# The order of all five instruction lists made anew in a chunk-selecting attention and ELU layer kernel

## The chip, the cores and the metric

The kernel runs on one core of one Trainium2 chip. The metric is the device time of one execution in microseconds, taken as the median of several runs. The engines of the core are called by short names: PE (TensorE, matmuls and transposes), ACT (ScalarE), DVE (VectorE), POOL (GpSimd) and SP (SyncE, which here only issues transfers). ACT and POOL issue transfers too, and such an issue is an instruction in the engine's own stream. Each engine works through its instructions in the order in which they stand and waits where an instruction needs what another engine or a transfer has not yet done.

## The reference

The first half is attention for 4 batches of 8 heads with 768 positions and 64 dimensions, in which each query attends to the six best of its allowed chunks of 32 keys:

```
k_min, k_max = min and max of each chunk of 32 keys
ub = sum(max(q * k_min, q * k_max), over the head's dimensions)
ub = where(chunk is not in the query's future, ub, -1e9)
top = the 6 chunks with the greatest ub
scores = where(key in a top chunk and not in the future, q @ k.T / 8, -1e9)
attn = softmax(scores);  x = attn @ v
```

The second half is a layer on the 3072 tokens with 512 features: `h = x @ w_in` (2048 wide), `g = where(h > 0, h, exp(min(h, 0)) - 1)`, and the result is `g @ w_out`, 3072 x 512 in float32.

## The kernel before, in words

Two heads make a pair; there are 16 pairs, four to a batch, and two pairs make a quad for the selection. Queries go in halves of 384. For a pair, k and q are brought into a layout with the head's 64 dimensions on the partitions, twice 64 for the two heads. DVE reduces each chunk of keys to its minimum and maximum; PE makes the bound `ub` from them (line 782); DVE finds the sixth greatest of each query (line 810) and marks the chunks below it (line 814), transposes the marks, and POOL puts them as extra rows below q (line 832). The extra rows of k hold an expanded identity times -40000, `econ` (line 531), copied there by DVE (line 542), so that one matmul (line 874) gives scores with the unwanted chunks pushed far down. ACT takes the exponential (line 901), PE multiplies with v (line 933), DVE divides by the sum (lines 946 and 949), PE transposes (line 982) and ACT copies the result into the tile xT (line 985). The second half takes xT: an up-projection in 16 pieces of 128 features (line 1011), the nonlinearity on ACT and DVE (lines 1020 to 1054), a down-projection (line 1070), a copy (line 1079) and a store (line 1084).

The first batch is prepared differently, to start early. `first_prep` loads k and q of a pair and half of the queries in plain rows (`load`, line 674) and v (line 679); PE transposes them, six instructions for a tile (`turn`, line 696), and ACT copies the transposed tiles out of PSUM (line 706 for k, 728 and 732 for q), while DVE reduces k from PSUM (line 715). Loads of k go through the queue of SP. The four loads of q for the first half of the queries are issued by ACT, all others of this batch by SP:

```
early = u - SPLIT[0] < EARLY[hf]
fetch(1, 256, 768, (pl + 0.1) - 300.0 * early, load(i0 + 1, qr, nc.scalar if early else nc.sync), [(sg, i0 + 1)],
      eng="ACT" if early else "SP")
```

The order of the work is written out by hand. The program first lists 1720 operations with what they read, write, allocate and free (`plan.add`), each with a number in the order of listing. The table `QUEUE` holds, for each of the five engines, these numbers in the order in which the engine is to do them. `Plan.order` walks through the five lists with assumed durations, latencies and transfer rates, and gives one common order and the buffer that each allocation takes; in that order the program is emitted (line 1115 and after), and semaphores are set between the engines from the tiles that they touch. The transfers of the SP and ACT queues share eight semaphores, used in turn in the order in which the built program has the transfers; a transfer whose semaphore is still in use by the transfer eight places earlier waits until that one has landed. The order of the built program follows the emission within each engine, while how ACT's and SP's transfers are put among each other also depends on what the building library takes the instructions of the two engines to last.

PSUM is shared out in banks: four banks are taken in turn by the transposed tiles, the up-projections, the outputs of attention and the down-projections (class `ps`, with counts for each kind), and two pairs of banks by the scores (class `S2`).

Of the kernel before, what the change touches and what calls it, by code (L numbers as in the profile page):

```python
# [73 lines left out]
    ],  # L74
    "POOL": [
# [10 lines left out]
    ],  # L86
    "ACT": [
# [19 lines left out]
    ],  # L107
# [7 lines left out]
    ],  # L115
# [1037 lines left out]
```

## Time and profile before

| what | before |
|---|---|
| median of 3 runs | 268.43 us (268.42 to 268.64) |
| span of the profiled execution | 266.7 us |
| PE busy | 256.0 us, 96% of the span |
| DVE busy | 211.6 us, 79% |
| ACT busy | 195.8 us, 73% |
| POOL busy | 118.0 us, 44% |
| moved by transfers | 32.15 MB, mean 121 GB/s |

A row of a stretch gives, for each engine, the time in which at least one of its instructions ran and their number. A row of the timeline gives start, duration, engine, line, operation, the tiles written and read, their shape, how many instructions are merged in it, and in brackets how long the engine had been idle and what ended that. "SPq" and "ACTq" are transfers issued by these engines. The matmuls overlap in PE, so the duration of one is longer than the distance to the next. The profiled execution's span is 1.7 us under the median of the runs.

### The profile page before, as it was taken

Reading aid. Unit: us, or ns where it says so; the run is one execution under the profiler, and the core shown is the slowest. Engines: PE = TensorE matmul, PEld = TensorE weight load, DVE = VectorE, ACT = ScalarE, POOL = GpSimd, SP = SyncE. Lnnn points to the kernel's source line nnn. Section 1 sums busy time; section 2 is a strip of 40 time slices with the busy share of each in tenths; the row PEclk is TensorE's granted clock in tenths of the full one; section 3 lists DMA queues with packets and bytes.
Section 4 is the critical chain, followed back from the end, with each engine's and each line's share of the span. In section 5 each row is a group of like instructions: output and inputs, shape, how many; then the busy total and the mean of one; then the engine's idle time right before and its main releaser. Section 6 shows DMA issues by size and latency. Waiting matters only on the chain.

```text
span 266.7 us, 6618 instructions
## 1 busy us (share of the span) xinstructions
PE 256.0 (96%) x2393; PEld 159.4 (60%) x2420; DVE 211.6 (79%) x544; ACT 195.8 (73%) x363; POOL 118.0 (44%) x208
## 2 busy tenths in 40 slices
PE   4999999999999999999999999999999999999994
PEld 3887766755565556655565555655666555565543
DVE  4897999999999999899997858986779676227640
ACT  4899899955987789997899549787988842433421
POOL 2588774163896898952934157524250000000000
PEclk9999999999999999999999999999999999999999
DMA  6999999999998999999403561040102300210123
GB/s 206 272 238 155 205 194 202 196 147 177 198 153 134 163 204 159 152 167 186 106 7 77 175 172 18 15 125 15 58 11 59 116 2 0 79 42 0 39 81 118
DMA packets 121264, 32.15 MB, mean 121 GB/s; under 512 B 108304, under 2 KB 118288, under 8 KB 121232
## 3 DMA queue, kind: packets, MB, share of 16 engines
q1 hardware_dynamic: 115920, 26.75, 51.3%
q0 software_dynamic: 4224, 4.19, 10.0%
q10 hardware_dynamic: 1088, 0.79, 0.9%
q8 instruction: 19, 0.31, 0.5%
q14 instruction: 13, 0.11, 0.2%
HBM read 28.44 MB, written 7.47 MB: 135 GB/s over the span
## 4 chain that ended last, share of the span: by engine, by line
PE 83%; DVE 5%; ACT 5%; DMA 4%; issue 2%; SPq 0%; DVEq 0%; ACTq 0%
PE psH L1011 20%; PE psM L1070 20%; PE psS L874 11%; PE psS L1011 8%; PE psMT L1070 8%; PE psO L933 7%; PE psS L782 3%; DMA f<-in_v_dram 3%; PE psH L696 2%; PE psMT L696 2%; ACT pt L901 2%; DMA gT<-in_k_dram 1%; ACT lhs L706 1%; PE psT L982 1%; DVE thr L810 1%
## 5 line engine op out<-in xcount | busy, mean ns | idle before, releaser
L901 ACT ACTIVATE pt<-psS 128x768 bf16<-128x768 f32 (+1 forms) x120 | 89.1, 778 | 11.9 <-PE psS L874 7.3
L1011 PE MATMUL psH<-xT,w_in_sb 128*128 128x384 bf16 x384 | 75.0, 326 | 0.3
L1070 PE MATMUL psM<-w_out_sb,gT 128*128 128x512 bf16 x264 | 67.9, 379 | 1.3
L1011 PEld LDWEIGHTS <-w_in_sb 128*128 128x128 bf16 x512 | 47.6, 97 | 34.4 <-issue 1.4
L1070 PEld LDWEIGHTS <-gT 128*128 128x128 bf16 x400 | 37.8, 98 | 34.4 <-DVE gT L1054 0.5
L1020 ACT ACTIVATE f<-psH 128x384 f32<-128x384 f32 x96 | 47.8, 509 | 12.5 <-PE psH L1011 10.1
L920 POOL TENSOR_SCALAR_AFFINE_SELECT pt<-pt 128x512 bf16<-128x512 bf16 (+1 forms) x48 | 24.8, 529 | 69.0 <-ACT pt L901 61.9
L874 PE MATMUL psS<-rhs,lhs 88*128 88x384 bf16 (+4 forms) x304 | 54.2, 283 | 0.8 <-ACT pt L901 0.6
L874 PEld LDWEIGHTS <-lhs 88*128 88x128 bf16 x304 | 27.9, 97 | 15.4 <-ACT pt L901 1.9
L1049 DVE SCALAR_TENSOR_TENSOR t<-f,psH 128x384 bf16<-128x384 f32 x56 | 30.5, 546 | 6.3 <-ACT f L1020 5.8
L748 POOL CAST rhs<-f 64x768 bf16<-64x768 f32 (+1 forms) x40 | 27.9, 702 | 14.1 <-DVE f L633 6.6
L933 PEld LDWEIGHTS <-pt 128*128 128x128 bf16 x672 | 27.5, 98 | 7.5 <-issue 0.9
L1054 DVE SCALAR_TENSOR_TENSOR gT<-psH,t 128x384 bf16<-128x384 f32 x56 | 30.6, 551 | 1.2
L933 PE MATMUL psO<-vext,pt 128*128 128x65 bf16 x672 | 29.6, 194 | 0.2 <-DVE gT L1054 0.2
L748 POOL CAST lhs<-f 64x768 bf16<-64x768 f32 x24 | 19.7, 822 | 18.6 <-PE psS L874 12.3
L832 POOL COPY rhs<-selt 24x576 bf16<-24x576 bf16 (+2 forms) x40 | 22.7, 567 | 8.6 <-DVE selt L821 5.8
L1020 ACT ACTIVATE f<-psS 128x768 f32<-128x768 f32 x16 | 13.0, 811 | 18.0 <-PE psS L1011 17.9
L1028 DVE SCALAR_TENSOR_TENSOR gT<-f,psH 128x384 bf16<-128x384 f32 x40 | 21.4, 542 | 5.3 <-ACT psH L1025 5.3
L1011 PE MATMUL psS<-xT,w_in_sb 128*128 128x384 bf16 x128 | 22.6, 326 | 0.0
L1070 PE MATMUL psMT<-w_out_sb,gT 128*128 128x512 bf16 (+1 forms) x109 | 22.1, 348 | 0.2
L1025 ACT ACTIVATE psH<-psH 128x384 f32<-128x384 f32 x40 | 20.7, 520 | 0.0
L949 DVE TENSOR_TENSOR on<-psO,rc 128x384 bf16<-128x384 f32 x32 | 17.6, 554 | 0.8
(56 smaller groups left out, 270.9 us busy)
## 6 DMA issues: line engine op xcount, KB each, us to landing
out_dram<-osb SPq DMA_DIRECT2D x23, 256.0 KB, 2.5
f<-in_k_dram SPq DMA_DIRECT2D x48, 96.0 KB, 3.9
f<-in_q_dram SPq DMA_DIRECT2D x48, 96.0 KB, 3.8
f<-in_v_dram SPq DMA_DIRECT2D x24, 192.0 KB, 4.0
w_in_sb<-in_moe_w_in_dram POOLq DMA_DIRECT2D x4, 512.0 KB, 7.9
w_out_sb<-in_moe_w_out_dram POOLq DMA_DIRECT2D x4, 512.0 KB, 8.4
gT<-in_k_dram SPq DMA_DIRECT2D x8, 192.0 KB, 4.4
gT<-in_v_dram SPq DMA_DIRECT2D x12, 128.0 KB, 3.9
```

Of the source, the lines that this page charges most:

```text
L748: nc.gpsimd.tensor_copy(out=o, in_=i)
L832: eng.tensor_copy(out=dst.rearrange("c h (i two x) -> c h i two x", two=2, x=32)[:, :, :, odd, :], in_=tiles[st][r0:r0 + NCH, c0:c0 + n].r ...
L874: nc.tensor.matmul(p_s[:, hd, pc:pc + w], lhsT=tiles[pt_["kb"]][0:64 + NCH, hd, 128 * kb:128 * kb + 128], rhs=tiles[pt_["qb"]][0:64 + NCH, ...
L901: lambda bs=bs, pt=pt, wtot=wtot, lo=lo, at=at: nc.scalar.activation(out=tiles[pt][:, :, lo:lo + wtot], in_=tiles[bs[0]][:, :, at:at + wto ...
L920: nc.gpsimd.affine_select(out=a, in_=a, compare_op=AOT.is_ge, fill=0.0, base=0, pattern=pat, channel_multiplier=-1)
L933: nc.tensor.matmul(po[:, hd, qi, :], lhsT=tiles[pt][:, hd, off:off + 128], rhs=tiles[pt_["vx"]][:, 6 * hd + kb, :], start=(kb == 0), stop= ...
L1011: nc.tensor.matmul(o, lhsT=w_in_sb[:, kk, f0:f0 + 128], rhs=rhs, start=(kk == 0), stop=(kk == NKK - 1))
L1020: lambda e=e, view=view: nc.scalar.activation(out=halves(e)[:, 0:step], in_=view(), func=AF.Exp),
L1028: lambda e=e, view=view, fc=fc, gt=gt: nc.vector.scalar_tensor_tensor(out=tiles[gt][:, fc:fc + step, :], in0=halves(e)[:, 0:step], scalar= ...
L1049: lambda e=e, t=t, view=view: nc.vector.scalar_tensor_tensor(out=tiles[t][:, 0:step], in0=halves(e)[:, 0:step], scalar=1.0, in1=view(), op ...
L1054: lambda t=t, view=view, fc=fc, gt=gt: nc.vector.scalar_tensor_tensor(out=tiles[gt][:, fc:fc + step, :], in0=view(), scalar=0.0, in1=tiles ...
L1070: nc.tensor.matmul(pm, lhsT=tiles[gt][:, fc, 128 * tt:128 * tt + 128], rhs=w_out_sb[:, fc, x0:x1], start=(fc == 0), stop=(fc == NFC - 1))
```

## The change: five new lists

All five lists of `QUEUE` are replaced. Each holds the same numbers as before, so every engine does the same operations, with the same shapes, on the same classes of buffers; the assumed lengths in `Plan` stay as they are. Of the 366 entries of ACT 339 stand elsewhere, of 562 of PE 528, of 382 of DVE 353, of 196 of POOL 180 and of 101 of SP 92; on average an entry moves by 4 (SP) to 9 (PE) places, at most by 55. The heads and tails of the lists show the kind of the moves:

```diff
     "ACT": [
-        15, 33, 49, 67, 2, 20, 21, 36, 37, 26, 27, 42, 43, 54, 55, 60, 61, 176, 70, 71, 177, 76, 77, 170, 171,
+        2, 33, 15, 49, 67, 20, 21, 36, 37, 42, 43, 70, 71, 26, 54, 27, 55, 60, 107, 108, 61, 76, 186, 187,
...
     "SP": [
-        13, 31, 163, 47, 65, 165, 17, 215, 181, 51, 217, 183, 197, 199, 201, 167, 517, 519, 534, 536, 551, 565,
+        13, 31, 163, 65, 47, 181, 183, 17, 165, 199, 215, 197, 51, 217, 519, 534, 167, 536, 517, 201, 551,
...
-        1341, 1704, 1697, 1711, 1718,
+        1270, 1658, 1644, 1263, 1355, 1697, 1711, 1704, 1718,
...
     "PE": [
-        19, 35, 25, 41, 53, 59, 175, 69, 81, 75, 169, 90, 185, 219, 191, 122, 203, 209, 106, 93, 131, 225, 147,
+        19, 35, 41, 69, 25, 53, 59, 106, 185, 75, 81, 90, 191, 169, 175, 122, 219, 147, 203, 131, 209, 225,
...
     "DVE": [
-        0, 6, 11, 9, 12, 8, 10, 22, 23, 38, 7, 39, 24, 40, 56, 57, 82, 72, 83, 73, 84, 172, 85, 58, 74, 188,
+        0, 8, 9, 11, 6, 12, 22, 10, 23, 24, 38, 39, 7, 40, 72, 73, 56, 57, 82, 83, 74, 84, 58, 188, 85, 189,
...
     "POOL": [
-        1, 5, 4, 3, 28, 29, 44, 45, 46, 62, 30, 63, 179, 78, 80, 79, 87, 64, 178, 86, 89, 195, 129, 194, 128,
+        1, 3, 5, 44, 45, 4, 28, 29, 30, 62, 46, 78, 79, 63, 195, 87, 64, 89, 194, 179, 178, 86, 88, 127,
```

In the ACT list 15, 33, 49 and 67 are the four loads of q, of pairs 0 to 3; 2 is econ; 20 and 21 copy the transposed k of pair 0, 36 and 37 that of pair 1. In the PE list 19 and 35 transpose k of pairs 0 and 1, 25 and 41 q of pairs 0 and 1, 53 and 69 k of pairs 2 and 3. In the SP list 13, 31, 47 and 65 load k of pairs 0 to 3, 17 is the first load of v, which has three parts, and the numbers from 163 to 217 are loads for the second half of the queries.

In the built program the first transfers stand as follows, with the semaphore that each waits for (the numbers in brackets are those of the lists; a value of 16 is one transfer landed, 32 two):

```
before                                   after
ACT q  (15)      no wait                 SP 13, 31, 163, 65, 47, 181, 183, and the
SP  k  (13)      no wait                    first part of 17: no wait (semaphores 0 to 7)
ACT q  (33)      no wait                 SP 17, parts 2 and 3    wait 0 >= 16, 1 >= 16
SP  k  (31)      no wait                 SP 165, 199             wait 2 >= 16, 3 >= 16
ACT q  (49)      no wait                 SP 215, 197             wait 4 >= 16, 5 >= 16
SP  k  (163)     no wait                 SP 51, part 1           wait 6 >= 16
ACT q  (67)      no wait                 ACT q (33)              wait 7 >= 16
SP  k  (47)      no wait                 SP 51, part 2           wait 0 >= 32
SP  k  (65)      wait 0 >= 16            ACT q (15)              wait 1 >= 32
SP  q  (165)     wait 1 >= 16            SP 51, part 3           wait 2 >= 32
SP  v  (17, 1)   wait 2 >= 16            ACT q (49)              wait 3 >= 32
...                                      ACT q (67)              wait 4 >= 32
```

On ACT itself the table load and econ stand first after the change, then the four loads of q, then the copies; before, the four loads stand first.

163 rows, old and new, of the table QUEUE are left out of this document.

## The prediction

> **What bounds the kernel now.** I read the page first, then the stretches by window, then the first microseconds as a timeline, engine by engine.
>
> ```profile
> span 266.7 us, 6618 instructions
> PE 256.0 (96%) x2393; PEld 159.4 (60%) x2420; DVE 211.6 (79%) x544; ACT 195.8 (73%) x363; POOL 118.0 (44%) x208
> PE 83%; DVE 5%; ACT 5%; DMA 4%; issue 2%; SPq 0%; DVEq 0%; ACTq 0%
> ```
>
> The profiled execution spans 266.7 us; the median of the three runs is 268.43 us, 1.7 us more, which lies around the span. I forecast a change of the span and add it to 268.43. TensorE (PE) is busy for 96% and makes 83% of the chain that ended last. What is left to win or lose is where PE is not the one that sets the pace. The stretches show where that is (columns: busy time of PE, PEld, DVE, ACT, POOL, then clock, DMA share and GB/s):
>
> ```profile
> 5.52:10.00 4.48, 4.46 (x26) 3.97 (x25) 4.45 (x14) 3.37 (x8) 1.25 (x3) 1.00 1.08 289
> 10.00:20.00 10.00, 9.54 (x150) 8.37 (x149) 8.44 (x38) 9.71 (x25) 7.73 (x18) 1.00 0.99 244
> 20.00:30.00 10.00, 9.25 (x180) 7.39 (x180) 8.27 (x45) 9.28 (x22) 8.93 (x18) 1.00 1.30 172
> 30.00:40.00 10.00, 9.79 (x100) 6.48 (x97) 9.52 (x18) 9.89 (x20) 7.05 (x13) 1.00 1.34 198
> 40.00:50.00 10.00, 9.95 (x93) 6.59 (x93) 9.47 (x20) 9.24 (x19) 4.15 (x6) 1.00 1.36 204
> 60.00:110.00 50.00, 49.39 (x462) 29.41 (x467) 49.44 (x129) 41.96 (x79) 38.68 (x60) 1.00 1.01 166
> 110.00:263.00 153.00, 152.01 (x1251) 89.53 (x1266) 111.09 (x251) 103.01 (x183) 44.05 (x73) 1.00 0.31 75
> 5.52:32.13 26.61, 25.34 (x377) 21.23 (x376) 23.25 (x99) 24.38 (x57) 19.73 (x39) 1.00 1.14 221
> ```
>
> Up to about 50 us ScalarE (ACT) is as full as PE: 9.71, 9.28, 9.89 and 9.24 us of each ten. From 60 to 110 us VectorE (DVE) is full, 49.44 of 50. After 110 us only PE is. So ACT is the engine that may not start late: what it loses at the start it can make up only from its own idle time. Between 5.52 us, its first copy of a transposed tile, and 32.13 us, the end of the copies that the first up-projection needs, that idle time is 26.61 - 24.38 = 2.23 us, of which 4.48 - 3.37 = 1.11 us lie before 10 us.
>
> The start itself, on ACT, then the load queue of SyncE (SPq), then PE:
>
> ```profile
> 0.80 2.06 ACTq L674 DMA_DIRECT2D gT<-in_q_dram  x4
> 2.90 1.28 ACT L531 ACT_TABLE_LOAD   x1 [2.90 <-issue]
> 4.20 0.84 ACT L531 ACTIVATE econ<-ident_f 32x768 bf16<-32x768 f32 x1
> 5.52 0.98 ACT L706 ACTIVATE lhs<-psH 64x384 bf16<-64x384 f32 x2 [0.48 <-PE psH L696]
> 30.66 1.47 ACT L985 ACTIVATE xT<-psT 128x384 bf16<-128x384 bf16 x3
> 31.44 1.71 PE L1011 MATMUL psH<-xT,w_in_sb 128*128 128x384 bf16 x8
> ```
>
> ```profile
> 4.29 0.37 SPq L674 DMA_DIRECT2D gT<-in_k_dram  x1
> 4.70 0.47 SPq L674 DMA_DIRECT2D gT<-in_q_dram  x1
> 5.42 0.37 SPq L679 DMA_DIRECT2D gT<-in_v_dram  x1
> 7.99 0.37 SPq L679 DMA_DIRECT2D gT<-in_v_dram  x1
> SPq L679 <- DMA gT<-in_q_dram: 1.9, 2, 1.6
> SPq L674 <- DMA gT<-in_q_dram: 1.5, 1, 1.5
> ```
>
> ```profile
> 3.96 2.79 PE L696 MATMUL psH<-ident_f,gT 128*128 128x128 f32 x12 [3.96 <-DMA gT<-in_k_dram]
> 9.13 0.85 PE L696 MATMUL psH<-ident_f,gT 128*128 128x128 f32 x6
> ```
>
> Two things are to be seen. ACT triggers four loads of q before anything else, free of any wait, and is done with that at 2.86 us. And no more than eight loads of the two queues are in flight: SP's load at 4.29 us is the ninth, and SP's rows of waits say that loads stood until an earlier load (of q) had landed, up to 1.6 us each. That is the built program's bookkeeping: eight semaphores used in turn, so that a load waits until the load eight places earlier has landed.
>
> **The change part by part.** Operations, shapes and tiles stay the same, so no duration is added or removed; only positions move. Four edits matter.
>
> *ACT's first five operations.* Before, the four q loads stand ahead of the expansion of the identity (econ, line 531); after, they stand behind it. In the built program that does more than the list says. While ACT loads its table (1.28 us) and makes econ (0.84 us), all eight semaphores go to SP's loads, and the four q loads become numbers 16, 18, 20 and 21 of the turn. The first waits for SP's 8th load, the second for its 10th, the third for its 12th, the fourth for its 13th. They are instructions of ACT, so every copy that ACT must make stands behind the fourth. When has SP's 13th load landed?
>
> ```profile
> gT<-in_k_dram SPq DMA_DIRECT2D x7, 192.0 KB, 4.0
> gT<-in_v_dram SPq DMA_DIRECT2D x4, 128.0 KB, 4.5
> DMA packets 4175, 2.34 MB, mean 234 GB/s; under 512 B 1601, under 2 KB 4175, under 8 KB 4175
> GB/s 0 0 0 0 0 0 0 58 49 240 221 320 369 363 375 363 372 301 255 273 280 301 286 258 249 320 363 366 363 363 356 351 318 306 269 224 203 206 236 170
> L674 ACTq DMA_DIRECT2D gT<-in_q_dram x4: 488/492/506, 0.8 to 2.4; - x4
> 10.00:11.00 1.00, 1.00 (x11) 1.00 (x10) 0.45 (x3) 0.97 (x2) 0.76 (x2) 1.00 1.01 273
> ```
>
> SP's first 13 loads are ten of 192 KB and three of 128 KB, together 2304 KB or 2.36 MB. In the trace of before the first 10 us moved 2.34 MB (the rows are for that stretch, in slices of 0.25 us), so the bytes alone take until 10.1 us. From the last byte to the end of the wait I take 0.8 us as an estimate: the slices sum to 0.4 MB, two loads, by 3.5 us, and the first waiting load went at 4.29 us. ACT's first two q loads are in flight by then and share the DMA engines; they are 0.39 MB, at 273 GB/s nothing to 1.4 us. The fourth trigger therefore goes between 10.9 and 12.3 us; I take the middle, 11.6. It takes 0.49 us itself, so ACT's first copy starts at 12.1 us instead of 5.52: 6.6 us later, with bounds 5.9 and 7.3.
>
> What hides it? Not another engine: the 61 ACT operations up to the last xT copy ahead of the first up-projection (line 1011, 31.44 us before) are the same set in both lists, so that row is due after the same ACT work. Of ACT's 2.23 us of idle time I let the early 1.11 us be made up (the transposes it waited for then will long be done) and keep the later 1.12 us, which came from waits for scores and selection that shift along. The delay at the first up-projection is 6.6 - 1.1 = 5.5 us.
>
> *PE's order behind that.* PE's third operation is now the transpose of the q tile that ACT's first held load brings, so PE stands from about 6.6 us (two groups of six transposes of k from 3.96 us, 2.79 us long) until that load lands, triggered near 7.8 us by the same byte count (SP's first eight loads, 1.5 MB, are reached at 7.0 us in the slices, and 0.8 us on top) and, at the 4 us from issue to landing of the rows above, landed near 12 us. From the fifth transpose on it needs PSUM banks that ACT's copies and DVE's reductions free, so ACT stays the later one; this costs nothing beyond the 5.5 us. Six transposes took 1.4 us in the first row of PE and 0.85 us at 9.13 us: the array may be slow again behind the gap, 0.55 us for each of the next two groups. They lie ahead of ACT's release, so I count 0, and 1.1 us for the upper end. [...]
>
> *DVE and POOL.* Econ is ready sooner (about 3 us instead of 5.04), so DVE's five copies of it, 2.77 us, run earlier:
>
> ```profile
> 5.07 2.77 DVE L542 COPY lhs<-econ 32x768 bf16<-32x768 bf16 x10 [2.71 <-ACT econ L531]
> 7.84 0.56 DVE L715 TENSOR_REDUCE km<-psH 128x12 f32<-128x384 f32 x1
> ```
>
> That saves nothing by itself, since the next operation, the reduction at 7.84 us, waits for ACT's second copy: 12.1 + 0.98 = 13.1 us, 5.3 us later than before. This is about the shift that PE sees, so DVE does not add to it. POOL (44% busy) waits for the same copies; 0, bounded by its idle time.
>
> *The rest of the five lists.* Most entries move by some five to nine places. After the first up-projection PE is idle for 0.21 + 0.05 us in the windows from 30 to 50, 0.61 us from 60 to 110 and 0.99 us from 110 to 263: 1.9 us is the most that a better order, or a delay taken up by waits that vanish, can give back; nothing is the least. I take 1.0. A loss here is possible where DVE is full (60 to 110 us), if its list asks for more before the same matmuls; I put 0 to 1.0 us, about the idle time seen there, and take 0. In the tail one store stands behind another that is ready later; the last matmuls, copies and the last store keep their order, so 0, up to 0.3 us.
>
> The sum: 6.6 - 1.1 - 1.0 = 4.5 us, 268.43 + 4.5 = 272.9 us.
>
> **The rivals.** *ACT is released early (the other side).* If the held loads cost ACT less than 2.2 us, that is if its first copy starts before about 7.7 us, its idle time takes it all, and the new order can win PE's idle time of 10 to 50 us, 0.46 + 0.75 + 0.21 + 0.05 = 1.5 us, and a little later: 266.9 us. For it speaks that q and k compete for the same engines and the sum of bytes is unchanged. Against it: 2.36 MB by 7.2 us would need 328 GB/s from the first instruction, and the trace has 234. [...] Chance 0.07.
>
> *The delay passes through whole.* ACT's waits all return at their old length and DVE, 5.3 us late, and the slow transposes add up to 1.1 us, with no gain later: 6.6 + 0 to 1.1, so 275.0 to 276.1 us. For it: up to 50 us both engines are over 90% full. Against it: 1.11 us of the idle time was waiting for the slow first transposes. Chance 0.2.
>
> *Most of it is taken up.* All of ACT's 2.23 us and PE's 1.9 us come back: 6.6 - 2.2 - 1.9 = 2.5 us, 270.9 us; with the early bound of the release 270.2. For it: the new lists could have been made with less waiting elsewhere. Against it: some of PE's idle is single gaps of 0.2 to 0.3 us that no order avoids. Chance 0.15.
>
> **How the numbers follow.** The forecast has 0.58 and its own range is 271.2 to 274.6 (release 10.9 to 12.3 us, idle made up between 1.1 and 3.0). The predicted time is 272.9 us. The range takes in the rivals on the slow side down to the early bound and up to the whole delay: 270.0 to 276.2. Outside stand the early release (0.07) and some 0.1 of worse cases. What a measurement of this kernel can tell from no change is about 0.2%, 0.54 us. Faster by more: 0.06; within: 0.03; slower: 0.91.
>
> **What would show it.** Right: the four q triggers on ACT come after econ and stretch to about 11 or 12 us, each behind a landing; ACT's first copy (line 706 moved by five) starts near 12 us; PE has a gap between about 6.6 and 12 us; the first up-projection starts near 37 us; behind 60 us PE is as full as before and the end comes about 4.5 us later. Wrong: the triggers go before 7 us, or the first up-projection starts near 37 us and the end is within 1 us of before, which would mean that PE's later time holds far more slack than its idle time shows; or losses of several us in the middle, which would mean that the order itself, not the start, decides.

## The result, and the profile after

| what | before | after |
|---|---|---|
| median | 268.43 us | 275.13 us (274.13 to 276.66, 4 runs) |
| profiled execution, its span | 268.4 us, 266.7 us | 274.13 us, 272.4 us |
| first up-projection starts | 31.44 us | 38.43 us |

The changed kernel is slower: the ratio of the times is 1.0248, with a 95% interval of 1.0207 to 1.0289. I had forecast 272.9 us in a range of 270.0 to 276.2; the sign and the range held, the value was 2.2 us too low. Two things make up most of that: the start lost 1.5 us more than I had summed, and the profiled execution, 274.13 us, lies 1.0 us under the median of the four. Where single executions of a kernel ran at a lower granted clock and some per cent longer than its others, the ratios below leave them out.

The page of the changed kernel has the same picture as before, with PE's share of the span down from 96% to 94% at the same busy time (255.5 us against 256.0):

```profile
span 272.4 us, 6614 instructions
PE 255.5 (94%) x2397; PEld 159.2 (58%) x2420; DVE 209.7 (77%) x544; ACT 194.4 (71%) x363; POOL 116.3 (43%) x208
```

So PE does no more work in all and stands longer. Where it stands is seen in the timeline of the start (start, duration, engine, line, operation, tiles, in brackets the idle time before and what ended it; all lines are five higher than before):

```profile
2.10 0.84 ACT L536 ACTIVATE econ<-ident_f 32x768 bf16<-32x768 f32 x1
3.60 2.79 PE L701 MATMUL psH<-ident_f,gT 128*128 128x128 f32 x12 [3.60 <-DMA gT<-in_k_dram]
...
8.43 3.39 ACTq L679 DMA_DIRECT2D gT<-in_q_dram  x4
11.86 1.99 ACT L711 ACTIVATE lhs<-psH 64x384 bf16<-64x384 f32 x4 [8.92 <-DMA gT<-in_k_dram]
12.94 0.56 DVE L720 TENSOR_REDUCE km<-psH 128x12 f32<-128x384 f32 x1 [6.76 <-issue]
13.27 1.54 PE L701 MATMUL psMT<-ident_f,gT 128*128 128x128 f32 x6 [6.88 <-DMA gT<-in_q_dram]
14.61 1.49 PE L701 MATMUL psH<-ident_f,gT 128*128 128x128 f32 x6
14.85 0.49 ACT L733 ACTIVATE f<-psMT 128x384 f32<-128x384 f32 x1 [1.00 <-PE psMT L701]
15.88 0.88 PE L701 MATMUL psMT<-ident_f,gT 128*128 128x128 f32 x6
16.13 0.98 ACT L711 ACTIVATE lhs<-psH 64x384 bf16<-64x384 f32 x2 [0.57 <-PE psH L701]
...
38.43 2.11 PE L1016 MATMUL psH<-xT,w_in_sb 128*128 128x384 bf16 x12
```

The view of waits for the first 40 us (engine, tile and line, waited for what: us in total, times, longest) gives two of these gaps their names:

```profile
ACT lhs L711 <- DMA gT<-in_k_dram: 8.9, 1, 8.9
PE psMT L701 <- DMA gT<-in_q_dram: 6.9, 1, 6.9
```

ACT makes econ and is done at 2.94 us. Its next instruction is the first trigger of a q load, which starts at 8.43 us; the four are through at 11.82 us, and only then come the copies of the transposed tiles, which had been waiting in PSUM since about 6.4 us. PE and DVE wait for the held load and the held copies. Behind the gap ACT waits twice more, 1.00 and 0.57 us, now for PE: the first two groups of six transposes there take 1.54 and 1.49 us.

Stretches of both kernels (length, then busy time and number of instructions of PE, PEld, DVE, ACT and POOL, then clock, DMA share, GB/s), of the changed kernel first: from ACT's first copy to its last xT copy, the middle, and from the first up-projection to the end. The last row is the kernel before from its first up-projection to the end.

```profile
11.86:38.54 26.68, 24.16 (x373) 20.40 (x374) 21.98 (x93) 24.24 (x57) 17.21 (x41) 1.00 1.18 180
60.00:110.00 50.00, 49.58 (x467) 29.48 (x471) 48.62 (x124) 39.75 (x72) 34.80 (x56) 1.00 0.99 153
38.43:272.00 233.57, 228.70 (x2018) 136.71 (x2038) 184.35 (x438) 168.18 (x306) 97.57 (x157) 1.00 0.57 105
```

```profile
31.44:266.70 235.26, 229.78 (x2016) 137.06 (x2040) 187.28 (x439) 169.84 (x307) 96.88 (x154) 1.00 0.57 108
```

The whole difference of the two spans can be laid out from these rows. ACT's first copy comes 11.86 - 5.52 = 6.34 us later. From there to the end of the last xT copy ACT takes 26.68 us, where it had taken 26.61 (the stretch from 5.52 to 32.13): 0.07 us more, with 57 instructions in both. The first up-projection starts 0.11 us ahead of that end, where it had started 0.69 us ahead: 0.58 us more. Then the rest takes 272.4 - 38.43 = 233.97 us instead of 235.26: 1.29 us less. The sum is 6.34 + 0.07 + 0.58 - 1.29 = 5.70 us, the difference of the two spans.

### The profile page after: what moved, and what is told of

The parts are those of the page before. It is cut to its first block, busy times and chain, and to the rows that moved or that the text cites. A ratio compares the mean times of both kernels' runs of the same rounds, so it can differ in the third digit from the quotient of the medians.

```text
span 272.4 us, 6614 instructions
## 1 busy us (share of the span) xinstructions
PE 255.5 (94%) x2397; PEld 159.2 (58%) x2420; DVE 209.7 (77%) x544; ACT 194.4 (71%) x363; POOL 116.3 (43%) x208
## 3 DMA queue, kind: packets, MB, share of 16 engines
HBM read 28.44 MB, written 7.47 MB: 132 GB/s over the span
## 4 chain that ended last, share of the span: by engine, by line
PE 88%; DMA 4%; ACT 3%; SPq 1%; DVE 1%; issue 1%; ACTq 0%; DVEq 0%
PE psH L1016 23%; PE psM L1075 22%; PE psS L879 13%; PE psO L938 7%; PE psMT L1075 6%; PE psS L1016 6%; PE psS L787 4%; PE psMT L701 2%; DMA gT<-in_q_dram 2%; PE psH L701 2%; ACT pt L906 2%; DMA gT<-in_v_dram 1%; PE psT L987 1%; SPq L679 1%; DMA out_dram<-osb 1%
## 5 line engine op out<-in xcount | busy, mean ns | idle before, releaser
L906 ACT ACTIVATE pt<-psS 128x768 bf16<-128x768 f32 (+1 forms) x120 | 89.8, 778 | 11.5 <-PE psS L879 10.5
L1075 PE MATMUL psM<-w_out_sb,gT 128*128 128x512 bf16 x267 | 69.7, 379 | 1.2 <-issue 0.2
L1025 ACT ACTIVATE f<-psH 128x384 f32<-128x384 f32 x96 | 46.7, 505 | 13.3 <-PE psH L1016 11.6
L879 PE MATMUL psS<-rhs,lhs 88*128 88x384 bf16 (+4 forms) x304 | 55.2, 283 | 0.7 <-ACT pt L906 0.6
L938 PEld LDWEIGHTS <-pt 128*128 128x128 bf16 x672 | 31.0, 98 | 10.3 <-issue 0.5
L938 PE MATMUL psO<-vext,pt 128*128 128x65 bf16 x672 | 34.9, 194 | 0.1
L879 PEld LDWEIGHTS <-lhs 88*128 88x128 bf16 x304 | 26.9, 98 | 13.2 <-issue 1.1
L1043 DVE TENSOR_SCALAR t<-f 128x768 bf16<-128x768 f32 x16 | 8.9, 557 | 17.3 <-ACT f L1025 17.3
## 6 DMA issues: line engine op xcount, KB each, us to landing
out_dram<-osb SPq DMA_DIRECT2D x23, 256.0 KB, 2.3
```

What stands on the lines that cost most here:

```text
L879: nc.tensor.matmul(p_s[:, hd, pc:pc + w], lhsT=tiles[pt_["kb"]][0:64 + NCH, hd, 128 * kb:128 * kb + 128], rhs=tiles[pt_["qb"]][0:64 + NCH, ...
L906: lambda bs=bs, pt=pt, wtot=wtot, lo=lo, at=at: nc.scalar.activation(out=tiles[pt][:, :, lo:lo + wtot], in_=tiles[bs[0]][:, :, at:at + wto ...
L938: nc.tensor.matmul(po[:, hd, qi, :], lhsT=tiles[pt][:, hd, off:off + 128], rhs=tiles[pt_["vx"]][:, 6 * hd + kb, :], start=(kb == 0), stop= ...
L1025: lambda e=e, view=view: nc.scalar.activation(out=halves(e)[:, 0:step], in_=view(), func=AF.Exp),
L1075: nc.tensor.matmul(pm, lhsT=tiles[gt][:, fc, 128 * tt:128 * tt + 128], rhs=w_out_sb[:, fc, x0:x1], start=(fc == 0), stop=(fc == NFC - 1))
```

## The experiments

My theory was that the loss comes from one entry: econ ahead of the four triggers, so that ACT stands in the turn of the eight semaphores and its copies stand behind it. The rivals were that the new lists lose by their order elsewhere, that the missing q data (and not the held ACT) set the time, that econ's place itself costs, and, for the size, that the transposes behind the gap matter. None of the kernels below leaves out a part of the work.

### The four triggers ahead of econ, in the new lists

```diff
     "ACT": [
-        2, 33, 15, 49, 67, 20, 21, 36, 37,
+        33, 15, 49, 67, 2, 20, 21, 36, 37,
```

> The changed lists, with the four q loads put back ahead of econ in ACT's list (33, 15, 49, 67, 2); nothing else is undone. Theory A (the held loads decide): the four triggers go free of waits by 2.9 us, ACT's first copy starts near 5.5 us instead of 11.86, the first up-projection near 31 to 32 us instead of 38.4, and the end comes some 6 to 7 us earlier than in the changed kernel: 267.0 to 268.6 us, level with before or up to 1.4 us faster, because behind the first up-projection the changed lists lost about 1.2 us less than those of before. Theory B (the new order as a whole asks too much of ACT and DVE early on): most of the loss stays, 272 us or more.

Measured: 269.07 us (268.64 to 269.51, 11 runs), ratio to the kernel before 1.0009 (0.9983 to 1.0034). The loss is gone with one entry moved: 275.13 - 269.07 = 6.1 us. The time is 0.5 us above the range that I had expected. The timeline, the start first and then the tail:

```profile
5.49 0.98 ACT L711 ACTIVATE lhs<-psH 64x384 bf16<-64x384 f32 x2 [0.46 <-PE psH L701]
10.41 0.87 PE L701 MATMUL psH<-ident_f,gT 128*128 128x128 f32 x6 [0.90 <-DVE kx L720]
32.80 2.11 PE L1016 MATMUL psH<-xT,w_in_sb 128*128 128x384 bf16 x12
...
235.45 0.60 ACT L1084 ACTIVATE osb<-psMT 128x512 f32<-128x512 f32 x1 [3.46 <-DMA out_dram<-osb]
238.45 2.99 PE L1016 MATMUL psS<-xT,w_in_sb 128*128 128x384 bf16 x16 [0.57 <-DVE gT L1048]
```

ACT's first copy is back at 5.49 us, and the first up-projection comes 5.6 us sooner than in the changed kernel, though 1.4 us later than in the kernel before. Two small losses of the new lists show now: at 10.41 us PE waits 0.90 us for a reduction of DVE, and at 235 us ACT's copy into osb waits for a store to free its buffer, with two exponentials queued behind it, and PE waits 0.57 us for what follows from them. Both are taken up below.

### Econ ahead of the triggers, in the old lists

```diff
     "ACT": [
-        15, 33, 49, 67, 2, 20, 21, 36, 37,
+        2, 15, 33, 49, 67, 20, 21, 36, 37,
```

> The lists of before, with only econ moved ahead of the four q loads in ACT's list (2, 15, 33, 49, 67). In the built program the four loads then wait for SP's 7th, 9th, 11th and 13th load. Theory A: ACT's first copy starts near 11.5 us, the first up-projection near 37 to 38 us, and the time is 273 to 276 us, the whole loss of the change from one moved entry. Theory B: 268 to 269.5 us.

Measured: 275.33 us (275.04 to 275.82, 4 runs), ratio 1.0248 (1.0232 to 1.0263). This one entry does alone what the whole change does. Its span is 274.1 us; its timeline:

```profile
8.18 4.51 ACTq L674 DMA_DIRECT2D gT<-in_q_dram  x4
12.74 1.99 ACT L706 ACTIVATE lhs<-psH 64x384 bf16<-64x384 f32 x4 [9.81 <-DMA gT<-in_q_dram]
38.91 1.71 PE L1011 MATMUL psH<-xT,w_in_sb 128*128 128x384 bf16 x8
```

The first copy is 7.22 us late, the first up-projection 7.47 us late, and the span 7.4 us longer. From the first up-projection to the end it takes 274.1 - 38.91 = 235.2 us, as in the kernel before (235.26). So the old lists give nothing of the delay back; the 1.3 us that the changed kernel gets back are not slack that any delay takes up, but need the new order.

### Two triggers ahead of econ, two behind

```diff
     "ACT": [
-        2, 33, 15, 49, 67, 20, 21, 36, 37,
+        33, 15, 2, 49, 67, 20, 21, 36, 37,
```

> The changed lists with the two q loads that PE needs first (33, 15) ahead of econ and the other two (49, 67) behind it. In the built program the third load waits for the 10th load in the common turn and the fourth for the 12th. So q of pairs 0 and 1 lands early, but ACT is still held until about 11 us. If what costs is that ACT stands behind the held triggers: first copy near 11 us, 273 to 275.5 us, at most 1.5 us less than the changed kernel. If what costs is that PE stands without q and its clock falls: PE has transposes to do from 3.6 us on, the gap goes, and most of the loss goes, 269 to 271 us.

Measured: 274.89 us (274.29 to 275.33, 4 runs), ratio 1.0233 (1.0218 to 1.0248). Here the q tiles that PE needs first are there in time, and PE goes on without a gap from 4.05 to 8.96 us, until its PSUM banks are full; ACT is still held by the other two triggers.

```profile
0.81 1.02 ACTq L679 DMA_DIRECT2D gT<-in_q_dram  x2
6.63 1.49 PE L701 MATMUL psMT<-ident_f,gT 128*128 128x128 f32 x6
9.15 1.52 ACTq L679 DMA_DIRECT2D gT<-in_q_dram  x2
10.71 1.99 ACT L711 ACTIVATE lhs<-psH 64x384 bf16<-64x384 f32 x4 [6.72 <-DMA gT<-in_v_dram]
13.81 1.51 PE L701 MATMUL psMT<-ident_f,gT 128*128 128x128 f32 x6 [4.84 <-DVE kx L720]
38.63 2.11 PE L1016 MATMUL psH<-xT,w_in_sb 128*128 128x384 bf16 x12
```

PE's gap ends at 13.81 us instead of 13.27, and what ends it is no longer a load but DVE's reduction, which waits for ACT's copies. The first up-projection is 0.2 us later than in the changed kernel. So the missing q is not what sets the time, and the standing of ACT, with what waits for its copies, keeps the whole loss. It does so by a longer way than the release alone: ACT's first copy is 1.15 us earlier here than in the changed kernel (10.71 against 11.86 us), but behind PE's gap three groups of transposes are slow (1.49 to 1.51 us), and ACT waits 1.06 and 0.79 us for two of them.

### The triggers on SP, econ first on ACT

```diff
-EARLY = (4, 0)
+EARLY = (0, 0)
...
     "ACT": [
-        2, 33, 15, 49, 67, 20, 21, 36, 37,
+        2, 20, 21, 36, 37,
...
     "SP": [
-        13, 31, 163, 65, 47, 181, 183, 17,
+        13, 31, 33, 65, 15, 47, 49, 67, 163, 181, 183, 17,
```

> The changed lists with econ still first on ACT, but the four q loads of the first half issued by SP, between its k loads (13, 31, 33, 65, 15, 47, 49, 67, 163 and so on as before), so that ACT triggers nothing and the loads hold the first eight semaphores. If the held triggers on ACT are the cause, and not that econ comes first: ACT's first copy near 5 to 5.5 us, 268.0 to 270 us. If econ and its table load in first place cost by themselves: 272 us or more.

Measured: 268.95 us over seven executions (267.24 to 269.85), ratio 0.9998 (0.9974 to 1.0021); three more took 274.41, 276.45 and 278.87 us. The profile is of the longest of these, so the start alone is compared. Econ stands first here as in the changed kernel, and the start is as early as before:

```profile
5.11 0.98 ACT L711 ACTIVATE lhs<-psH 64x384 bf16<-64x384 f32 x2 [2.17 <-PE psH L701]
30.93 0.81 PE L1016 MATMUL psH<-xT,w_in_sb 128*128 128x384 bf16 x4
```

ACT has nothing to trigger, so no landing holds it, and the first up-projection, at 30.93 us, is 0.5 us earlier than in the kernel before. Econ's place by itself costs nothing; behind it, it is the trigger that costs. Moving the triggers to SP is not shown to be safe, though. This long execution loses its time after the start, as the waits from 10 to 70 us show:

```profile
POOL vext L744 <- DMA gT<-in_v_dram: 12.8, 3, 10.5
PE psO L938 <- POOL vext L744: 8.0, 1, 8.0
```

POOL waited 10.5 us for a load of v, and PE 8.0 us for POOL. The page's row of the granted clock has 5 and 7 tenths in its slices from 48.5 to 62.4 us, at the end of this wait and behind it, and 9 in all others. Whether the two other long executions had the same wait, and whether the new place of the loads brings it about, is not known.

### The transposes behind the gap kept fast

```diff
             def f():
                 p_ = ps(bb, [P, HALF], F32)
+                if i == 3 and bb is bq and sg == STAGED[0]:
+                    for _ in range(40):
+                        nc.tensor.transpose(p_[:, 0:P], ident_f, ident_f)
                 for n in range(3):
```

> The kernel after the change, with 40 transposes of the identity more on PE, put into the gap ahead of the first held q tile and into the bank that this tile's transpose then overwrites: work that has no use, added so that PE does not stand idle from 6.4 to 13.3 us. The result is the same. At 0.14 to 0.23 us each they end near 12 us, ahead of the landing of q, so they delay nothing. If the slow transposes behind the gap (1.54 and 1.49 us for six instead of 0.82) are what my sum left out, the groups now take 0.82 to 0.88 us, the first up-projection starts 0.7 to 1.4 us sooner (37.0 to 37.7 instead of 38.4 us), the time is 273.5 to 274.5 instead of 275.1, and single runs differ by less than the 2.5 us of the kernel after. If the slow transposes are covered by ACT's copies, as my prediction had it, the groups are short but the up-projection starts within 0.3 us of 38.4 and the time stays at 274.8 to 275.4.

Measured: 274.05 us (273.67 to 274.60, 5 runs), ratio to the kernel before 1.0211 (1.0197 to 1.0225). Its lines are three higher in this part than in the changed kernel.

```profile
5.84 6.13 PE L700 MATMUL psMT<-ident_f 128*128 128x128 f32 x40
11.95 1.99 ACT L714 ACTIVATE lhs<-psH 64x384 bf16<-64x384 f32 x4 [9.01 <-DMA gT<-in_q_dram]
13.01 0.88 PE L704 MATMUL psMT<-ident_f,gT 128*128 128x128 f32 x6 [1.04 <-DMA gT<-in_q_dram]
13.72 0.82 PE L704 MATMUL psH<-ident_f,gT 128*128 128x128 f32 x6
13.97 0.49 ACT L736 ACTIVATE f<-psMT 128x384 f32<-128x384 f32 x1
37.56 2.11 PE L1019 MATMUL psH<-xT,w_in_sb 128*128 128x384 bf16 x12
41.83 1.48 PE L1019 MATMUL psH<-xT,w_in_sb 128*128 128x384 bf16 x8 [1.03 <-DMA w_in_sb<-in_moe_w_in_dram]
11.95:37.67 25.72, 23.06 (x374) 19.27 (x374) 21.88 (x93) 24.32 (x57) 17.24 (x41) 1.00 1.09 175
```

With PE kept at work in the gap, the groups of six take 0.88 and 0.82 us where they took 1.54 and 1.49, ACT copies the first q tile at 13.97 us without a wait, and the first up-projection comes 0.87 us sooner, although PE does 40 transposes more. The last row, again the stretch from ACT's first to its last copy, shows how: ACT's idle time in it is 25.72 - 24.32 = 1.40 us, where the changed kernel has 26.68 - 24.24 = 2.44. The load that ends PE's gap landed 0.26 us earlier here (13.01 against 13.27 us), which may account for up to that much; the rest, some 0.6 us at least, is the transposes. So the slow transposes were on the path. How much of it reaches the end is less sure: the medians differ by 1.1 us, but the runs of the two kernels overlap (273.67 to 274.60 and 274.13 to 276.66 us), and the two profiled spans differ by only 0.4 us, with a new wait of 1.03 us for a load of weights at 41.83 us in this one.

### The changed kernel once more

Its four runs lay 2.5 us apart, those of the kernel before 0.2. One more execution of the same kernel was profiled:

> The changed kernel once more, for a second look: its four runs lay near 274.2 (two) and near 276.3 us (two). If the same mode comes, 274.2 and the same first 20 us; if the other, 276.3 us, and the difference of 2 us should show in the first 35 us, either as slow transposes (1.5 us for six instead of 0.85) for one more stretch behind the gap, or as later landings of q.

Measured: 275.2 us, span 273.5.

```profile
12.24 1.99 ACT L711 ACTIVATE lhs<-psH 64x384 bf16<-64x384 f32 x4 [9.31 <-DMA gT<-in_k_dram]
13.75 1.54 PE L701 MATMUL psMT<-ident_f,gT 128*128 128x128 f32 x6 [7.43 <-DMA gT<-in_q_dram]
15.08 1.49 PE L701 MATMUL psH<-ident_f,gT 128*128 128x128 f32 x6
16.36 1.49 PE L701 MATMUL psMT<-ident_f,gT 128*128 128x128 f32 x6
39.62 2.11 PE L1016 MATMUL psH<-xT,w_in_sb 128*128 128x384 bf16 x12
```

Against the first profile ACT is released 0.38 us later, a third group of transposes is slow (1.49 instead of 0.88 us), and the first up-projection starts 1.19 us later; the span is 1.1 us longer. So the difference between these two runs is made in the start, by the landing of the loads and by how many groups are slow. For the slowest of the runs, 276.66 us, there is no profile.

### The triggers first, and one store's copy later

This is the first experiment's kernel with one more entry moved, in the tail of ACT's list: operation 1650, the copy that waited for a store, goes behind the two exponentials.

```diff
     "ACT": [
-        2, 33, 15, 49, 67, 20, 21, 36, 37,
+        33, 15, 49, 67, 2, 20, 21, 36, 37,
...
-        1347, 1650, 1661, 1673, 1340,
+        1347, 1661, 1673, 1650, 1340,
```

> As the run with the q loads ahead of econ (269.07 us), and in ACT's list the copy of a result (1650) is moved behind the two exponentials 1661 and 1673. In that run PE stood 0.73 us at 238 us, while ACT stood 3.5 us before that copy, until a store had given its buffer free, and the two exponentials waited behind it. If that is the whole of the loss in the tail: 0.7 to 1.0 us less, 268.1 to 268.4 us. If PE's lost time only moves to the next wait: 268.8 us or more.

Measured: 268.24 us (267.91 to 268.49, 12 runs), ratio 0.998 (0.9968 to 0.9992).

```profile
33.22 2.11 PE L1016 MATMUL psH<-xT,w_in_sb 128*128 128x384 bf16 x12
235.26 0.60 ACT L1084 ACTIVATE osb<-psMT 128x512 f32<-128x512 f32 x1
237.94 0.60 ACT L1084 ACTIVATE osb<-psM 128x512 f32<-128x512 f32 x1 [2.09 <-DMA out_dram<-osb]
```

The moved copy, at 235.26 us, has no wait any more: ACT does the two exponentials first, and by then the store has freed the buffer. The wait for a store is left at the next copy (operation 1340, at 237.94 us), 2.09 us long, and nothing that PE needs stands behind that one. The span is 266.6 us. From the first up-projection to the end it takes 266.6 - 33.22 = 233.4 us instead of 267.5 - 32.80 = 234.7 in the first experiment.

### And DVE's zero fill put back

The same kernel, and in DVE's list the setting to zero of rows below q (operation 6, 1.05 us) second again, as in the old list:

```diff
     "DVE": [
-        0, 8, 9, 11, 6, 12, 22,
+        0, 6, 8, 9, 11, 12, 22,
```

> The new lists with the four q loads first on ACT and the last osb copy behind the two exponentials (268.24 us), and one entry of the DVE list put back: the setting to zero (operation 6, 1.05 us, line 542) second instead of fifth, so that DVE does it while it waits for econ. Theory: PE's wait of 0.9 us near 10.4 us for DVE's reduction is then gone, ACT is the later engine from there on, and the first up-projection starts 0.3 to 1.0 us sooner than 33.2; 267.2 to 267.9 us. Rival: the start is set by ACT's copies and the bytes alone, the wait moves to another tile, and the time stays at 268.0 to 268.5.

Measured: 266.94 us (266.89 to 267.00, 5 runs), ratio to the kernel before 0.9940 (0.9928 to 0.9953): faster than both kernels.

```profile
1.30 1.05 DVE L542 MEMSET rhs<- 32x192 uint32 x5
9.33 0.84 PE L701 MATMUL psMT<-ident_f,gT 128*128 128x128 f32 x6 [0.50 <-DMA gT<-in_q_dram]
31.84 2.11 PE L1016 MATMUL psH<-xT,w_in_sb 128*128 128x384 bf16 x12
```

DVE fills the rows while it waits for econ, its reductions come sooner, and PE's wait for DVE near 10 us is gone. The first up-projection comes 1.38 us sooner, a little more than I had expected, and all of that reaches the end (span 265.2 instead of 266.6 us). The medians differ by 1.3 us; the two kernels were run in different batches, and by their ratios to the kernel before it is 1.1 us. Against the kernel before, the first up-projection is 0.4 us later, and the rest takes 265.2 - 31.84 = 233.4 us instead of 235.3. These 1.9 us are not the new lists' alone: with only the triggers put first they take 234.7 us for this stretch, 0.6 us less than the old lists, and the other 1.3 us came with the move of one store's copy.

### The old lists' start joined to the new lists' rest

The question was whether the gain behind the start is the new order's own. The lists were cut behind the first 340 operations in the old common order and went on in the order of the kernel of the section before the last (triggers first, one store's copy later). On SP and DVE the seam looks like this:

```diff
     "SP": [
         13, 31, 163, 47, 65, 165, 17, 215, 181, 51, 217, 183, 197, 199, 201, 167, 517, 519, 534, 536, 551,
-        565, 568, 570, 553, 531, 548,
+        568, 553, 570, 531, 548,
...
     "DVE": [
...
-        257, 358, 258, 370, 365, 366, 386, 381,
+        257, 358, 258, 538, 539, 540, 370, 544,
```

> The order of before up to about 41 us (the first 340 operations as emitted, 75 of DVE, 79 of ACT, 84 of PE), the changed order of everything else, and the same move in the tail. In the run with the q loads first PE had lost 1.0 us more than before by its 31st us of work, and from there to its 222nd us lost 1.2 us where before lost 2.4. If that smaller loss is the new order's own: 1.0 to 1.5 us under before, 267.0 to 267.6 us. If it is only the later start that left DVE time to run ahead: PE loses it again between 60 and 110 us, and the time is level with before, 268.2 to 268.8 us.

Measured: six executions from 274.00 to 283.50 us, all of them longer than any of the kernel before in the same batch (at most 270.09 us). The ratio, from the two shortest (274.00 and 278.05 us), is 1.0273 (1.0211 to 1.0334). The seam itself made a new wait. The view of waits from 40 to 52 us in the execution of 278.05 us has it (lines are four higher than before):

```profile
PE psO L937 <- DVE gT L1058: 5.9, 1, 5.9
DVE f L637 <- DMA f<-in_q_dram: 4.7, 1, 4.7
```

DVE reaches a copy of loaded q before that load has landed, and what PE needs next stands behind it on DVE. This run does not answer its question, which stays open. As a case it shows the same pattern once more: an in-order engine that is asked early for something that a transfer brings late.

## Why the prediction was right or wrong

**Econ ahead of the triggers: right, and sized well.** I had the fourth trigger at 11.6 us and the first copy at 12.1 us, from the bytes of SP's first thirteen loads and 0.8 us on top; the first copy came at 11.86 us, at 12.24 us in the same kernel's second profile, and at 12.74 us in the old lists with econ first. That the one entry makes the whole loss is shown by putting it back (6.1 us gone) and by moving it alone in the old lists (6.7 us, 275.33 against 268.60 in the same batch). That it is not econ's place as such is shown by the kernel with the triggers on SP, and that it is not the missing q by the kernel with two triggers first, where ACT was held all the same.

**ACT's early idle time made up, -1.1 us: wrong.** This is the term that was mis-sized most. ACT idled 2.44 us between its first and its last copy, not less than the 2.23 us before: nothing was made up. I had argued that the transposes it waited for would long be done. Two groups were; the next two came behind PE's gap and took 1.54 and 1.49 us, and ACT waited 1.00 and 0.57 us for them. I had seen that they might be slow and set them at 0, because I took them to lie ahead of ACT's release. That did not follow even from my own times, a landing near 12 us and a release at 12.1 us. And the load that ended PE's gap landed at 13.27 us, not near 12: its trigger came at 8.43 us instead of 7.8, and it was 4.84 us on its way. I had taken 4 us from the loads of k, where the loads of q that ACT issues had a median of 5.1 us in the trace of before. With the groups kept fast the idle time was 1.40 us, 0.83 us less than before, near the 1.1 us of my term. What the runs show of the slow groups is this: the first groups behind gaps of 4.84, 6.05, 6.88 and 7.43 us took 1.51 to 1.54 us for six, and those behind gaps of 0.90 and 1.04 us took 0.87 and 0.88. For a gap between 1.04 and 4.84 us that is not shown, and neither is what sets the number of slow groups: one profile of the changed kernel has two, the other three.

**The first up-projection near 37 us: too early.** It came at 38.43: 1.5 us more than summed, of which 1.17 us are the term above (-1.1 forecast, +0.07 measured) and 0.58 us are the first up-projection's place behind the xT copies, which I had taken as unchanged; the release was 0.24 us earlier than summed.

**Something given back behind it, -1.0 us: the size right (1.29 us), the reason half right.** I had allowed for two: a better order, or waits that vanish in the delay. The old lists with the same delay gave back less than 0.1 us, so a delay alone gives nothing. From the first up-projection to the end the kernel before takes 235.3 us. The new lists take 234.0 and 233.9 us in the two profiles of the changed kernel, 234.7 in the kernel with two triggers first, 234.7 without the delay (first experiment), and 233.4 without it and with one store's copy moved. What sets these apart, as far as the traces show it, is not the delay but one wait of PE for DVE in the tail, behind the copy that waits for a store: 0.24 and 0.2 us in the changed kernel, 0.9 and 0.57 us in the two kernels at 234.7, none where the copy is moved. So the gain is the order's, 0.6 to 1.9 us by the length of that wait. The loss that I feared for the stretch from 60 to 110 us did not come: DVE is at 48.62 us there instead of 49.44.

**The tail, 0 to 0.3 us: near that in the changed kernel, more elsewhere.** In the first experiment's kernel, with the tail of the new lists, moving one copy was worth 0.8 us of the median (269.07 to 268.24). I had looked at the last stores and not at what a store holds when its copy stands ahead of two exponentials. In the changed kernel ACT waits 3.14 us before the same copy, and PE loses 0.24 us behind it; the move itself was not tried there.

**DVE: right with ACT late, wrong in general.** I counted the moves on DVE's list at nothing since its reductions wait for ACT's copies. That holds while ACT is held (DVE stood idle for 6.76 us before its first reduction in the changed kernel). With ACT released at 5.5 us, the place of a 1.05 us fill was worth 1.1 to 1.3 us.

**The rivals.** The early release fell: the waits are for landings, and moving one entry cost 6.7 us. What the triggers take to issue did not set the price: four triggers on ACT take 2.06 us when free and 3.39 us when each waits for a landing, and ACT stood for 8.9 us in all before its first copy. The rival that the delay passes through whole, with slow transposes on top, was the better account of the start, and the median lies in its 275.0 to 276.1 us, though the changed kernel does get something back later. My own case, 271.2 to 274.6 us, holds the profiled execution and not the median. I gave that rival 0.2 and held against it that 1.11 us of ACT's idle time had been waiting for the slow first transposes; the gap made two more slow groups, and ACT's copies did not hide them. Two sums of mine were off beside this: the lower end of my own range comes to 271.3 and not 271.2 us, and the chances of the forecast and the three rivals add to 1.00, which left no room for the 0.1 of worse cases.

**The spread of the runs** was not in the prediction at all. The two profiles of the changed kernel, 1.1 us apart, differ in when loads land and in how many groups are slow behind the gap; for the rest of the 2.5 us there is no profile.

## What to carry to other kernels

When a transfer is triggered by an engine that also computes, look up which earlier transfer its semaphore waits for: the wait holds everything behind it on that engine (ACT's first copy started 6.34 us later here), and one place in a list can decide whether the trigger is among the first eight or the twenty-first. Sum a delay from the landing that ends it, and look at what PE does in the meantime: if it stands for several microseconds (4.8 to 7.4 us here), count its next instructions at the slow rate (1.5 us for six transposes here, instead of 0.82 to 0.88) and ask whether someone waits for them. A new order is best judged with its worst wait taken away first; here the new lists were 2.5% slower as they came, level with the old ones with the triggers put first, and 0.6% faster with two more entries moved.

## What the runs showed that I had not expected

The row of the granted clock did not always tell here whether PE was slow. In the changed kernel the row for the slow groups says 1.00; in the kernel with two triggers first it says 0.50 for groups that take the same 1.5 us:

```profile
13.27:15.88 2.61, 2.61 (x12) 2.40 (x13) 2.55 (x8) 1.28 (x4) 0.48 (x1) 1.00 1.15 293
```

```profile
13.81:16.40 2.59, 2.59 (x13) 2.37 (x14) 2.09 (x6) 0.98 (x2) 1.30 (x7) 0.50 1.25 244
```

The durations were the safer witness for these stretches of 2.6 us.

The runs of the changed kernel lay 2.5 us apart, where those of the kernel before lay 0.2 us apart in the same batch, those of the kernel with the gap filled 0.9 us and those of the best one 0.1 us. That the gap makes runs less steady is not shown by this: the old lists with econ first have a gap of 6.05 us and four runs only 0.8 us apart, and in other batches the kernel before had runs up to 3.8 us apart.
